# One expert of a mixture-of-experts kernel: half blocks chained on five PSUM banks, last outputs by accumulating DMAs, last products reordered

## The chip, the cores and the metric

The kernel runs on one core of a Trainium2 chip. The core has a matrix engine (TensorE, PE in the profile, with its weight loads as PEld), a vector engine (DVE), a scalar engine (ACT), a general engine (POOL) and a queue engine (SP); each runs its own instructions in order and waits for the others on semaphores. Matrix products land in PSUM, which the kernel uses in banks of 512 fp32 numbers per partition. The metric is the device time of one execution in microseconds; three runs of the kernel before took 2339.73, 2339.75 and 2340.48 us, with a median of 2339.75 us.

## What is computed

The output is the sum of three parts over 2048 tokens of 512 channels: the input, a state-space convolution of the normalized input (by an FFT in the reference), and a mixture of eight experts, of which all eight are taken for every token. Cut to what matters here:

```python
for e in range(E):
    mask = (topk_idx == e)
    w = (gates * mask).sum(-1, keepdims=True)
    h = _silu(xf @ w1[e]) @ w2[e]
    out = out + w * h
return x + _A_ref(xn, ...) + out
```

Each `w1[e]` is 512 by 1792 and each `w2[e]` is 1792 by 512. This case is about the last expert, e = 7.

## The kernel before, in words

Numbers are held as two fp16 halves (high and low), so that one exact product is three matmuls: high by high, high by low, low by high. On top of that the products are cut in a 2 by 2 scheme with seven block products in place of eight (Strassen's, in Winograd's form), with sums of blocks made before and after. For experts 0 to 6 only the first layer is done so. For the last expert (`strong` in the code) the second layer, too, is done with seven products, numbered 1 to 7.

**Blocks and slots.** The tokens go in four token blocks (`tb` 0 to 3) of 512. For the last expert each token block has two half blocks (`a` = 0, 1), and a half block is computed by two calls of `block2` (`d` = 0, 1 for the first half block, 2, 3 for the second): one for four of the seven pairs of hidden features (`prs` 0 to 3), one for the other three (4 to 6). A call of `block2` issues the first layer in four slots, s = 0 to 3: one first-layer product in slot 0, two in each of the others, in three PSUM banks A, B, C (`hb`). A product of one pair is 6 matmuls of 128 columns (L1775). Slot 1 ends with the copy of B to C on ACT (L1872), the activation of A (`act11`), and `act12` of the call before; slot 2 keeps C and A in SBUF (`keep`, L1785), and POOL adds the two with an accumulating DMA (L1666).

**From activation to second layer.** Each of the seven left operands of the second layer is scaled to fp16 on ACT (`high`, L1803) and gets its low half on DVE (`low`, L1808). Some are sums of activations, made by DVE (`total`, L1814). `when(n, f)` puts a step off by n slots; `flush()`, at the end of each slot, runs the steps that are due. When `low` is issued, one unit per pair is appended to the list `units` of that half block. A unit is one second-layer product of one pair: three matmuls of 256 columns (L1701). A half block has 7 products of 7 pairs, 49 units. Counted in slots from the start of the first call of a half block, a unit can be taken from this slot on: product 1 from slot 3, 4 from slot 6, 2 and 7 from 7, 5 and 6 from 8, 3 from 9 (four pairs each); those of the second call (three pairs each) four slots later, so that the last three, of product 3, come in slot 13. That is slot 1 of the second call of the next half block.

**`pop2`** takes up to 7 units in each slot, after the slot's first-layer products and ahead of its `flush()`. It takes half blocks strictly in order. When the 49th unit is taken it calls `evacuate2` and stops, and the slot behind it stays without units (`gap`). The seven accumulators lie in four banks, y0 to y3, the same for each half block.

**`evacuate2`** copies product 1 to SBUF on ACT (L1717), forms the four output blocks with seven DVE additions (L1719 to L1728), and one slot later scales them by the gates on ACT (L1733) and adds them to the sums in DRAM with accumulating DMAs on POOL (L1735); five slots later SP copies the finished rows to the output (L1737). For both half blocks of the last token block it does otherwise: the sums were loaded to SBUF beforehand (`final_load`, L1660), DVE multiplies by the gates and adds (L1745 to L1756), and SP and ACT issue the output DMAs themselves (L1744). Its instructions are issued inside `pop2`, and so ahead of what `flush()` issues in that slot.

```python
        if (e, tb) in strong:
            pop2(pops)
        else:
            pop(pops)
        flush()
```

**Preparation of the weights** (`work_on`) is a list of steps that a slot may take one or two of; each step is mostly one scaling on ACT (L493) and one low half on DVE (L496). At e = 6 and 7, once the memory of the convolution is free, each slot takes up to two more (L1641).

Of the kernel before, what the change touches and what calls it, by code (L numbers as in the profile page):

```python
# [9 lines left out]
F32 = mybir.dt.float32  # L10
# [4 lines left out]
ALU = mybir.AluOpType  # L15
# [3 lines left out]
P = 128  # L19
# [14 lines left out]
def s4_moe_kernel(  # L34
# [15 lines left out]
    nc = tc.nc  # L50
    V, S, T = nc.vector, nc.scalar, nc.tensor

    NTOK, D = u.shape
    NT = NTOK // P
    KT = D // P
    E, NPR = w1.shape[0], w1.shape[1]
    NF = 2 * NPR
    TB = 512
    NB = NTOK // TB
    TPB = TB // P  # L60
    TH = TB // 2
# [527 lines left out]
    second_half = {}  # L589
# [51 lines left out]
    def work_on(limit):  # L641
        clock["two"], n2 = False, limit
        while limit > 0:
            fetch()
            it = None
            for n, c in enumerate(work[:6]):
                if c.load is None:
                    if n == 0 and can(c):
                        it = c
                        break  # L650
                    if n == 0 and (c.e, c.w, 0) in done:
                        continue
                    break
                if c.raw is not None and can(c):
                    it = c
                    break
            if it is None:
                break
            if it.sums and len(it.steps) == it.n:
                live["tw"], it.at = True, now()  # L660
            low = it.steps.pop(0)(it.raw)
            limit -= 1
            clock["two"] = limit == 0 and n2 == 2
            last = not it.steps
            if last:
                work.remove(it)
            if low:
                lows.append((low, last, it.sums and last, it.made))
            elif last and it.load is not None:
                live["n"] -= 1  # L670
        fetch()
# [350 lines left out]
    def at_(n):  # L1022

        return n / 1050 + 0.17

    def tt_(n):

        return n / 960 + 0.1
# [6 lines left out]
    def now():  # L1035
        return clock["slot"]
# [481 lines left out]
    def when(n, f):  # L1518
        todo.append((now() + n, f))
# [97 lines left out]
    def slot(e, tb, d, s, pops):  # L1617
        for f in mid.get((e, tb, d, s), ()):
            f()
        if e + tb == 0:  # L1620
            work_lows()
# [5 lines that stand above are left out]
        if e == 0:  # L1627
            work_lows()
        room = act_room()
        if room > 1.0 and run_later():  # L1630
            room -= 1.6
        for f in side.get((e, tb, d, s), ()):
            f()
        work_lows()
        if e + tb == 0 or tb == NB - 1:
            work_on(2 if e + tb == 0 or room > 2 and (e or d < 3) else 1)
        elif e == 0 and tb == 1:
            work_on(2 if (d, s) < (2, 1) else 1 if (d, s) == (2, 1) else 0)
        elif room > 1.0:
            work_on(1 if room < 2.2 or e else 2)  # L1640
        if "pool" in second_half and e >= E - 2 and work:  # L1641
            work_on(2)
        if (e, tb, d, s) >= (0, 2, 3, 1):
            if (e, tb, d, s) == (0, 2, 3, 1):
                clock["pe"] = clock["pe0"] = clock["pe1"] = clock["dve"] = clock["dve0"] = 0.0
            bg_run()
        if "s4" in done and "pool" not in second_half:
            open_second()
        clock["slot"] += 1
# [19 lines left out]
    order2 = [(e, tb, a) for e in range(E) for tb in range(NB) if (e, tb) in strong for a in range(2)]  # L1669
    gap = {"at": -1}  # L1670
    OPS = (0, 3, 1, 2, 4, 5, 6)
    BANKS = {1: (0, 0), 6: (0, 1), 5: (1, 0), 7: (1, 1), 4: (2, 0), 2: (3, 0), 3: (3, 1)}

    def w2_op(pr, p, b):
        c = {1: (0, 0), 2: (1, 0), 3: (1, 1)}.get(p)
# [4 lines left out]
    def pop2(n):  # L1680

        while n > 0 and units:
            pop(1)
            n -= 4
        while n > 0 and order2 and now() > gap["at"]:
            key = order2[0]
            ps = passes.get(key)
            if ps is None or not ps["units"]:
                break
            e, pr = key[0], ps["units"][0][0]  # L1690
            if (True, (e, "w2", pr)) not in made or (True, (e, "w2x", pr)) not in made:
                break
            pr, q, p, t = ps["units"].pop(0)
            bank_, half = BANKS[p]
            first = bank_ not in ps["y"]
            if first:
                ps["y"][bank_] = ps_y.tile([P, 2, TH], F32, tag=f"y{bank_}", name=f"z{e}_{key[1]}_{key[2]}_{bank_}")
            acc = ps["y"][bank_][:, half, :]
            c = ps["n"][p] = ps["n"].get(p, 0) + 1
            for k, (a, b) in enumerate(((0, 0), (0, 1), (1, 0))):  # L1700
                T.matmul(acc, t[:, a, q, :], w2_op(pr, p, b), start=(first and k == 0), stop=(c == NPR and k == 2),  # L1701
                         skip_group_check=True)
            clock["pe"] += 0.325
            n -= 1
            ps["left"] -= 1
            if ps["left"] == 0:
                order2.pop(0)
                gap["at"] = now() + 1
                evacuate2(*key, {p: ps["y"][b][:, h, :] for p, (b, h) in BANKS.items()})
                n = 0  # L1710

    def evacuate2(e, tb, a, y):
        i0, i1 = tb * TPB + a, tb * TPB + a + 2
        g0, g1 = gates_e[e][:, i0:i0 + 1], second_half["gneg"][:, i1:i1 + 1]
        ev = second_half["pool"].tile([P, 3, TH], F32, tag="ev", name=f"ev{e}_{tb}_{a}", bufs=1)
        t1, v, w = ev[:, 0, :], ev[:, 1, :], ev[:, 2, :]
        S.copy(t1, y[1])  # L1717
        clock["act"] += at_(TH)
        V.tensor_tensor(v, t1, y[6], op=ALU.subtract)  # L1719
        V.tensor_tensor(w, v, y[5], op=ALU.add)  # L1720
        clock["dve"] += 7 * tt_(TH)
        if (e, tb) != (E - 1, NB - 1):
            o = [sb.tile([P, 2, TH], F32, tag="stg", name=f"ye{e}_{i}", bufs=4) for i in (i0, i1)]
            V.tensor_tensor(o[0][:, 0, :], t1, y[2], op=ALU.add)
            V.tensor_tensor(o[1][:, 1, :], w, y[7], op=ALU.add)
            V.tensor_tensor(v, v, y[7], op=ALU.add)
            V.tensor_tensor(o[1][:, 0, :], v, y[4], op=ALU.add)
            V.tensor_tensor(o[0][:, 1, :], w, y[3], op=ALU.add)  # L1728

            def send():  # L1730
                for i, t, g in ((i0, o[0], g0), (i1, o[1], g1)):
                    t = t.rearrange("p a d -> p (a d)")
                    S.activation(t, t, AF.Copy, scale=g)  # L1733
                    clock["act"] += at_(D)
                    nc.gpsimd.dma_start(oacc[i], t, accum_op=ALU.add)  # L1735
                    if e == E - 1:
                        when(5, lambda i=i: nc.sync.dma_start(out[i * P:(i + 1) * P, :], oacc[i]))  # L1737
            when(1, send)
            return
        f0, f1 = stg[i0], stg[i1]  # L1740
        lo, hi = slice(0, TH), slice(TH, D)

        def send(i, c, q):
            q.dma_start(out[i * P:(i + 1) * P, c], stg[i][:, c])  # L1744
        V.scalar_tensor_tensor(f0[:, lo], t1, g0, f0[:, lo], op0=ALU.mult, op1=ALU.add)  # L1745
        V.scalar_tensor_tensor(f0[:, hi], w, g0, f0[:, hi], op0=ALU.mult, op1=ALU.add)
        V.tensor_tensor(w, w, y[7], op=ALU.add)
        V.scalar_tensor_tensor(f1[:, hi], w, g1, f1[:, hi], op0=ALU.mult, op1=ALU.add)
        send(i1, hi, nc.scalar)
        V.tensor_tensor(v, v, y[7], op=ALU.add)  # L1750
        V.tensor_tensor(v, v, y[4], op=ALU.add)
        V.scalar_tensor_tensor(f1[:, lo], v, g1, f1[:, lo], op0=ALU.mult, op1=ALU.add)
        send(i1, lo, nc.sync)
        V.scalar_tensor_tensor(f0[:, lo], y[2], g0, f0[:, lo], op0=ALU.mult, op1=ALU.add)
        send(i0, lo, nc.sync)
        V.scalar_tensor_tensor(f0[:, hi], y[3], g0, f0[:, hi], op0=ALU.mult, op1=ALU.add)  # L1756
        send(i0, hi, nc.scalar)

    def block2(e, tb, d):
# [1 line left out]
        a, prs = d // 2, ((0, 1, 2, 3), (4, 5, 6))[d % 2]  # L1761
        n = len(prs)
        key = (e, tb, a)
        ps = passes.setdefault(key, {"units": [], "y": {}, "n": {}, "left": 7 * NPR})
        A, B, C = (h.rearrange("p a t -> p (a t)").rearrange("p (q t) -> p q t", q=4) for h in hb)
        tk = slice(a * P, (a + 1) * P)
        last = d == 3
# [119 lines left out]
        prod(B, 6, 2)  # L1887
        sB = keep("scB", B)
        add(sB[:, :n], sE[:, :n])
        if (e, tb) == (E - 1, NB - 1) and d in (1, 3):  # L1890
            for j in (d // 2, d // 2 + 2):
                final_load(j)
        slot(e, tb, d, 3, pops[3])
        later.append(lambda: act22(sC))
# [113 lines left out]
    while later or todo or order2:  # L2008
        if later:
            later.pop(0)()  # L2010
        pop2(10)
        flush()
        clock["slot"] += 1

# [55 lines left out]
```

## Time and profile before

| what | us |
|---|---|
| median of three runs (2339.73 to 2340.48) | 2339.75 |
| time of the profiled execution | 2341.02 |
| its span in the profile | 2339.2 |
| PE busy | 2308.1 |
| DVE busy | 1851.9 |
| ACT busy | 1503.5 |
| POOL busy | 339.5 |
| first matmul of the last expert's first layer starts at | 2043.6 |
| first matmul of its second layer starts at | 2074.04 |
| its last matmul starts at | 2331.9 |

The profiled execution took 2341.02 us, of which the span, from the first to the last thing that the profiler recorded, is 2339.2 us. Times below are counted from the start of the span. "Idle before" in the profile is the time in which an engine did nothing ahead of an instruction, with what ended it behind an arrow. A row with x36 stands for 36 instructions of one kind.

### The profile page before, as it was taken

Reading aid. Unit: us, or ns where it says so; the run is one execution under the profiler, and the core shown is the slowest. Engines: PE = TensorE matmul, PEld = TensorE weight load, DVE = VectorE, ACT = ScalarE, POOL = GpSimd, SP = SyncE. Lnnn points to the kernel's source line nnn. Section 1 sums busy time; section 2 is a strip of 40 time slices with the busy share of each in tenths; the row PEclk is TensorE's granted clock in tenths of the full one; section 3 lists DMA queues with packets and bytes.
Section 4 is the critical chain, followed back from the end, with each engine's and each line's share of the span. In section 5 each row is a group of like instructions: output and inputs, shape, how many; then the busy total and the mean of one; then the engine's idle time right before and its main releaser. Section 6 shows DMA issues by size and latency. Waiting matters only on the chain.

```text
span 2339.2 us, 49749 instructions
## 1 busy us (share of the span) xinstructions
PE 2308.1 (99%) x19969; PEld 1614.2 (69%) x19969; DVE 1851.9 (79%) x3737; ACT 1503.5 (64%) x2650; POOL 339.5 (15%) x396
## 2 busy tenths in 40 slices
PE   8999999999999999999999999999999999999997
PEld 4666666666666666666666666666666666689997
DVE  8864889989998999888999889998999734645444
ACT  7676666656666576665766667666666656756663
POOL 0010101121111211101111011110111101131110
PEclk9999999999999999999999999999999999999999
DMA  8597356665576655745556555565555755675442
GB/s 275 181 266 194 95 148 155 142 125 111 125 172 134 132 116 123 168 114 119 114 124 157 123 116 121 118 158 122 121 111 125 158 118 141 160 136 110 96 93 60
DMA packets 326457, 320.24 MB, mean 137 GB/s; under 512 B 183696, under 2 KB 221072, under 8 KB 325776
## 3 DMA queue, kind: packets, MB, share of 16 engines
q1 hardware_dynamic: 269776, 222.91, 32.9%
q0 software_dynamic: 55872, 93.61, 25.5%
q8 instruction: 156, 2.56, 0.4%
q14 instruction: 77, 0.63, 0.1%
q10 hardware_dynamic: 576, 0.52, 0.1%
HBM read 205.55 MB, written 66.06 MB: 116 GB/s over the span
## 4 chain that ended last, share of the span: by engine, by line
PE 82%; issue 7%; DVE 3%; DMA 3%; ACT 3%; POOL 1%; SPq 0%; DVEq 0%; POOLq 0%; ACTq 0%
PE hb L1463 32%; PE y L1446 12%; PE y L1448 12%; PE y L1447 12%; PE hb L1775 6%; PE z L1701 5%; DMA scC<-sE 1%; PE kgen L854 1%; PE uf L921 1%; PE kf L935 1%; PE yp L1009 1%; ACT ye L1421 0%; ACT ahl L1483 0%; POOL oacc L1424 0%; DVE ahl L1492 0%
## 5 line engine op out<-in xcount | busy, mean ns | idle before, releaser
L1463 PE MATMUL hb<-xop,w1s 128*128 128x256 f16 x7938 | 934.3, 273 | 5.0 <-ACT scC L1924 3.4
L1463 PEld LDWEIGHTS <-w1s 128*128 128x128 f16 x7938 | 766.2, 98 | 151.5 <-issue 9.4
L1447 PE MATMUL y<-w2s,ahl 128*128 128x512 f16 x1568 | 595.0, 379 | 0.4 <-DVE w2s L496 0.4
L1446 PE MATMUL y<-w2s,ahl 128*128 128x512 f16 x1568 | 595.1, 380 | 0.0
L1448 PE MATMUL y<-w2s,ahl 128*128 128x512 f16 x1568 | 595.0, 379 | 0.0
L1666 POOL DMA_DIRECT2D scC<-sE x124 | 114.8, 926 | 1352.5 <-ACT sE L1924 1036.6
L1448 PEld LDWEIGHTS <-ahl 128*128 128x128 f16 x1568 | 153.4, 98 | 185.6 <-issue 0.7
L1447 PEld LDWEIGHTS <-ahl 128*128 128x128 f16 x1568 | 153.4, 98 | 140.5
L1446 PEld LDWEIGHTS <-ahl 128*128 128x128 f16 x1568 | 153.4, 98 | 140.4
L1479 ACT ACTIVATE fa<-hb,sc 128x512 f32<-128x512 f32 (+1 forms) x220 | 140.0, 636 | 153.3 <-PE hb L1463 152.6
L1492 DVE SCALAR_TENSOR_TENSOR ahl<-fa,sc,ahl 128x512 f16<-128x512 f32 (+1 forms) x230 | 157.1, 683 | 52.9 <-ACT ahl L1483 52.5
L1939 ACT COPY hb<-hb 128x512 f32<-128x512 f32 x108 | 55.9, 517 | 196.9 <-PE hb L1463 196.7
L1666 POOL DMA_DIRECT2D scB<-sE x124 | 107.3, 865 | 390.3 <-ACT scB L1924 253.9
L1483 ACT ACTIVATE ahl<-fa,sc 128x512 f16<-128x512 f32 (+1 forms) x230 | 154.4, 672 | 8.9 <-DMA xnd<-xn 1.5
L1775 PE MATMUL hb<-xop,w1s 128*128 128x128 f16 x2352 | 143.6, 221 | 6.7 <-ACT scC L1785 6.6
L1775 PEld LDWEIGHTS <-w1s 128*128 128x128 f16 x2352 | 138.1, 99 | 10.1 <-issue 6.9
L1492 DVE SCALAR_TENSOR_TENSOR ahl<-scB,sc,ahl 128x512 f16<-128x512 f32 x108 | 73.6, 681 | 81.3 <-ACT ahl L1483 79.9
L842 DVE TENSOR_TENSOR tb<-ta,tt 128x64 f32<-128x64 f32 (+2 forms) x192 | 132.0, 687 | 5.7
L836 DVE TENSOR_TENSOR ta<-tb,zr 128x64 f32<-128x64 f32 (+2 forms) x192 | 131.7, 686 | 5.3
L1929 ACT COPY hb<-hb 128x512 f32<-128x512 f32 x108 | 56.0, 519 | 122.9 <-PE hb L1463 122.1
L976 DVE TENSOR_TENSOR s<-s,tm 128x672 f32<-128x672 f32 (+6 forms) x224 | 127.8, 571 | 7.7
L839 DVE TENSOR_TENSOR tt<-tb,zi 128x64 f32<-128x64 f32 (+2 forms) x192 | 130.5, 679 | 0.0
(319 smaller groups left out, 3220.7 us busy)
## 6 DMA issues: line engine op xcount, KB each, us to landing
xop<-xd SPq DMA_DIRECT2D x210, 256.0 KB, 4.0
pp<-in_w_dram SPq DMA_DIRECT2D x98, 512.0 KB, 4.3
raw<-in_w_dram SPq DMA_DIRECT2D x63, 512.0 KB, 4.9
oacc<-ye POOLq DMA_DIRECT2D x108, 256.0 KB, 6.0
scC<-sE POOLq DMA_DIRECT2D x89, 256.0 KB, 4.2
scB<-sE POOLq DMA_DIRECT2D x89, 256.0 KB, 4.1
raw<-in_w_dram SPq DMA_DIRECT2D x52, 256.0 KB, 3.5
raw<-in_w_dram SPq DMA_DIRECT2D x104, 128.0 KB, 3.5
```

Of the source, the lines that this page charges most:

```text
L836: V.tensor_tensor(ta, tin, zrv, op=ALU.mult)
L839: V.tensor_tensor(tt, tin[:, ::-1], ziv, op=ALU.mult)
L842: V.tensor_tensor(tout, ta, tt, op=ALU.add)
L1446: T.matmul(y, lhs[0], w2s[pr][:, 0, fh, :], start=(c == 0), stop=False)
L1447: T.matmul(y, lhs[0], w2s[pr][:, 1, fh, :], start=False, stop=False)
L1448: T.matmul(y, lhs[1], w2s[pr][:, 0, fh, :], start=False, stop=(c == NF - 1))
L1463: T.matmul(dst[:, q, :], w1s[pr][:, a, wo, k * P:(k + 1) * P], xop[:, xo, b, k, :], start=(first_mm and q == 0 and n == 0), stop=(n == 5), ...
L1479: S.activation(fa, src[:, :n], AF.Silu, scale=w1_unscale(e, d if whole else prs[0]))
L1483: S.activation(ahl[:, 0, :n], fa, AF.Copy, scale=scales[e][:, 3:4])
L1492: V.scalar_tensor_tensor(ahl[:, 1, :n], fa, sc[:, 3:4], ahl[:, 0, :n], op0=ALU.mult, op1=ALU.subtract)
L1666: nc.gpsimd.dma_start(dst, src, accum_op=ALU.add)
L1775: T.matmul(dst[:, q, :], w1s[pr][:, x, (0, 1, 2, 3, 6, 5, 4)[wo], k * P:(k + 1) * P], xop[:, xo, b, k, tk], start=(first_mm and q == 0 and ...
```

## The change

Eight edits, all in the last expert but the first, which also concerns expert 6:

1. In a slot of experts 6 and 7, `work_on` takes one more step in place of two.
2. `pop2` no longer stops when a half block is done. In the same slot it goes on with units of the next half block that go to its bank 0 (products 1 and 7); from the slot behind it on, it takes any unit. The same holds where the last units of expert 6 run out.
3. The accumulators go round five banks (`bank_tile`): half block number n has its four banks shifted by 4n modulo 5. The fifth is the bank "s4" that the convolution used. Products 1 and 7 share bank 0, 4 and 5 bank 1, 6 has bank 2, 2 and 3 share bank 3.
4. `evacuate2` copies bank 0 whole (products 1 and 7, 512 columns) in one ACT instruction; the DVE additions take product 7 from SBUF, and keep their temporaries in the output tiles. There are seven of them as before, in another order.
5. The first half block of the last token block leaves by the accumulating DMAs, as the others do; its output DMAs follow after three slots.
6. For the very last half block (`LAST`) units of product 2 are taken only when there are no others, and those of product 3 last of all; product 3 has the fifth bank to itself.
7. `final_load` loads the sums of the last half block alone, both in slot 3 of d = 1.
8. Behind the last slot, `pop2` takes 4 units at a step in place of 10.

```diff
         if "pool" in second_half and e >= E - 2 and work:
-            work_on(2)
+            work_on(1)
...
-    BANKS = {1: (0, 0), 6: (0, 1), 5: (1, 0), 7: (1, 1), 4: (2, 0), 2: (3, 0), 3: (3, 1)}
+    LAST = order2[-1]
+    RANK = {2: 1, 3: 2}
+
+    def half_of(key, p):
+        b, h = {1: (0, 0), 7: (0, 1), 4: (1, 0), 5: (1, 1), 6: (2, 0), 2: (3, 0), 3: (3, 1)}[p]
+        return (4, 0) if (key, p) == (LAST, 3) else (b, h)
+
+    def bank_tile(key, b):
+        n = (4 * passes[key]["n"] + b) % 5
+        return (ps_y if n else ps_s).tile([P, 2, TH], F32, tag=f"y{n - 1}" if n else "s4", name=f"z{key[0]}_{key[1]}_{key[2]}_{b}")
...
         while n > 0 and units:
             pop(1)
             n -= 4
-        while n > 0 and order2 and now() > gap["at"]:
+            if not units:
+                gap["at"] = now()
+                n = min(n, 4)
+        while n > 0 and order2:
             key = order2[0]
-            ps = passes.get(key)
-            if ps is None or not ps["units"]:
+            ps, e = passes.get(key), key[0]
+            if ps is None:
                 break
-            e, pr = key[0], ps["units"][0][0]
-            if (True, (e, "w2", pr)) not in made or (True, (e, "w2x", pr)) not in made:
+            ok = [u for u in ps["units"] if (now() > gap["at"] or half_of(key, u[2])[0] == 0)
+                  and (True, (e, "w2", u[0])) in made and (True, (e, "w2x", u[0])) in made]
+            if not ok:
                 break
-            pr, q, p, t = ps["units"].pop(0)
-            bank_, half = BANKS[p]
+            if key == LAST:
+                ok.sort(key=lambda u: RANK.get(u[2], 0))
+            pr, q, p, t = ok[0]
+            ps["units"].remove(ok[0])
+            bank_, half = half_of(key, p)
...
             if ps["left"] == 0:
                 order2.pop(0)
-                gap["at"] = now() + 1
-                evacuate2(*key, {p: ps["y"][b][:, h, :] for p, (b, h) in BANKS.items()})
-                n = 0
+                gap["at"] = now()
+                evacuate2(*key, {p: ps["y"][half_of(key, p)[0]][:, half_of(key, p)[1], :] for p in range(1, 8)}, ps["y"][0])
...
-        ev = second_half["pool"].tile([P, 3, TH], F32, tag="ev", name=f"ev{e}_{tb}_{a}", bufs=1)
-        t1, v, w = ev[:, 0, :], ev[:, 1, :], ev[:, 2, :]
-        S.copy(t1, y[1])
-        clock["act"] += at_(TH)
+        ev = second_half["pool"].tile([P, 2, TH], F32, tag="ev", name=f"ev{e}_{tb}_{a}", bufs=1)
+        t1, t7 = ev[:, 0, :], ev[:, 1, :]
+        S.copy(ev, both)
...
         V.tensor_tensor(v, t1, y[6], op=ALU.subtract)
         V.tensor_tensor(w, v, y[5], op=ALU.add)
-        clock["dve"] += 7 * tt_(TH)
-        if (e, tb) != (E - 1, NB - 1):
-            o = [sb.tile([P, 2, TH], F32, tag="stg", name=f"ye{e}_{i}", bufs=4) for i in (i0, i1)]
+        if (e, tb, a) != LAST:
+            V.tensor_tensor(v, v, t7, op=ALU.add)
+            V.tensor_tensor(v, v, y[4], op=ALU.add)
+            V.tensor_tensor(o[1][:, 1, :], w, t7, op=ALU.add)
             V.tensor_tensor(o[0][:, 0, :], t1, y[2], op=ALU.add)
-            V.tensor_tensor(o[1][:, 1, :], w, y[7], op=ALU.add)
-            V.tensor_tensor(v, v, y[7], op=ALU.add)
-            V.tensor_tensor(o[1][:, 0, :], v, y[4], op=ALU.add)
-            V.tensor_tensor(o[0][:, 1, :], w, y[3], op=ALU.add)
+            V.tensor_tensor(w, w, y[3], op=ALU.add)
...
-                        when(5, lambda i=i: nc.sync.dma_start(out[i * P:(i + 1) * P, :], oacc[i]))
+                        when(5 if tb < NB - 1 else 3, lambda i=i: nc.sync.dma_start(out[i * P:(i + 1) * P, :], oacc[i]))
...
-        if (e, tb) == (E - 1, NB - 1) and d in (1, 3):
-            for j in (d // 2, d // 2 + 2):
+        if (e, tb) == (E - 1, NB - 1) and d == 1:
+            for j in (1, 3):
                 final_load(j)
...
-        pop2(10)
+        pop2(4)
```

More of the change, by code (lines that the diff above doesn't have):

```diff
@@ L1684, in pop2 @@
             n -= 4
-        while n > 0 and order2 and now() > gap["at"]:
+            if not units:
+                gap["at"] = now()
+                n = min(n, 4)
+        while n > 0 and order2:
             key = order2[0]
-            ps = passes.get(key)
-            if ps is None or not ps["units"]:
+            ps, e = passes.get(key), key[0]
+            if ps is None:
                 break
-            e, pr = key[0], ps["units"][0][0]
-            if (True, (e, "w2", pr)) not in made or (True, (e, "w2x", pr)) not in made:
+            ok = [u for u in ps["units"] if (now() > gap["at"] or half_of(key, u[2])[0] == 0)
+                  and (True, (e, "w2", u[0])) in made and (True, (e, "w2x", u[0])) in made]
+            if not ok:
                 break
-            pr, q, p, t = ps["units"].pop(0)
-            bank_, half = BANKS[p]
+            if key == LAST:
[3 more added lines that the diff above has]
+            bank_, half = half_of(key, p)
             first = bank_ not in ps["y"]
             if first:
-                ps["y"][bank_] = ps_y.tile([P, 2, TH], F32, tag=f"y{bank_}", name=f"z{e}_{key[1]}_{key[2]}_{bank_}")
+                ps["y"][bank_] = bank_tile(key, bank_)
             acc = ps["y"][bank_][:, half, :]
-            c = ps["n"][p] = ps["n"].get(p, 0) + 1
+            c = ps["c"][p] = ps["c"].get(p, 0) + 1
             for k, (a, b) in enumerate(((0, 0), (0, 1), (1, 0))):
@@ L1707, in pop2, with evacuate2 @@
                 order2.pop(0)
-                gap["at"] = now() + 1
-                evacuate2(*key, {p: ps["y"][b][:, h, :] for p, (b, h) in BANKS.items()})
-                n = 0
-    def evacuate2(e, tb, a, y):
+                gap["at"] = now()
+                evacuate2(*key, {p: ps["y"][half_of(key, p)[0]][:, half_of(key, p)[1], :] for p in range(1, 8)}, ps["y"][0])
+    def evacuate2(e, tb, a, y, both):
         i0, i1 = tb * TPB + a, tb * TPB + a + 2
         g0, g1 = gates_e[e][:, i0:i0 + 1], second_half["gneg"][:, i1:i1 + 1]
-        ev = second_half["pool"].tile([P, 3, TH], F32, tag="ev", name=f"ev{e}_{tb}_{a}", bufs=1)
-        t1, v, w = ev[:, 0, :], ev[:, 1, :], ev[:, 2, :]
-        S.copy(t1, y[1])
-        clock["act"] += at_(TH)
+        ev = second_half["pool"].tile([P, 2, TH], F32, tag="ev", name=f"ev{e}_{tb}_{a}", bufs=1)
+        t1, t7 = ev[:, 0, :], ev[:, 1, :]
+        S.copy(ev, both)
+        clock["act"] += at_(D)
+        clock["dve"] += 7 * tt_(TH)
+        o = [sb.tile([P, 2, TH], F32, tag="stg", name=f"ye{e}_{i}", bufs=4) for i in (i0, i1)]
+        v, w = o[1][:, 0, :], o[0][:, 1, :]
         V.tensor_tensor(v, t1, y[6], op=ALU.subtract)
         V.tensor_tensor(w, v, y[5], op=ALU.add)
-        clock["dve"] += 7 * tt_(TH)
-        if (e, tb) != (E - 1, NB - 1):
-            o = [sb.tile([P, 2, TH], F32, tag="stg", name=f"ye{e}_{i}", bufs=4) for i in (i0, i1)]
+        if (e, tb, a) != LAST:
+            V.tensor_tensor(v, v, t7, op=ALU.add)
+            V.tensor_tensor(v, v, y[4], op=ALU.add)
+            V.tensor_tensor(o[1][:, 1, :], w, t7, op=ALU.add)
             V.tensor_tensor(o[0][:, 0, :], t1, y[2], op=ALU.add)
-            V.tensor_tensor(o[1][:, 1, :], w, y[7], op=ALU.add)
-            V.tensor_tensor(v, v, y[7], op=ALU.add)
-            V.tensor_tensor(o[1][:, 0, :], v, y[4], op=ALU.add)
-            V.tensor_tensor(o[0][:, 1, :], w, y[3], op=ALU.add)
+            V.tensor_tensor(w, w, y[3], op=ALU.add)
             def send():
@@ L1746, in evacuate2 @@
         V.scalar_tensor_tensor(f0[:, hi], w, g0, f0[:, hi], op0=ALU.mult, op1=ALU.add)
-        V.tensor_tensor(w, w, y[7], op=ALU.add)
+        V.tensor_tensor(w, w, t7, op=ALU.add)
         V.scalar_tensor_tensor(f1[:, hi], w, g1, f1[:, hi], op0=ALU.mult, op1=ALU.add)
         send(i1, hi, nc.scalar)
-        V.tensor_tensor(v, v, y[7], op=ALU.add)
+        V.tensor_tensor(v, v, t7, op=ALU.add)
         V.tensor_tensor(v, v, y[4], op=ALU.add)
@@ L1763, in block2 @@
         key = (e, tb, a)
-        ps = passes.setdefault(key, {"units": [], "y": {}, "n": {}, "left": 7 * NPR})
+        ps = passes.setdefault(key, {"units": [], "y": {}, "c": {}, "left": 7 * NPR, "n": len(passes)})
         A, B, C = (h.rearrange("p a t -> p (a t)").rearrange("p (q t) -> p q t", q=4) for h in hb)
```

## The prediction

> **What bounds the kernel now.** I read the page first, then the waits of PE in the last expert, then the stretches between them, then the slots by the timeline.
>
> ```profile
> span 2339.2 us, 49749 instructions
> PE 2308.1 (99%) x19969; PEld 1614.2 (69%) x19969; DVE 1851.9 (79%) x3737; ACT 1503.5 (64%) x2650; POOL 339.5 (15%) x396
> PE hb L1775 <- ACT scC L1785: 6.6, 2, 5.3
> PE z L1701 <- ACT ye L1421: 2.3, 1, 2.3
> PEld L1701 <- DVE hs L1808: 1.6, 6, 0.3
> 2140.00:2170.00 30.00, 29.99 (x408) 28.12 (x406) 15.76 (x29) 18.23 (x33) 5.23 (x6) 1.00 0.41 76
> ```
>
> The first two lines are the page's: PE is busy for 99% of the span. The next three are waits within the last expert (total, times, longest). In the last row the second number is PE's busy time in 30 us in its middle: none is idle, at full clock (1.00). So the free slot costs nothing there: PE fills it with first-layer products. The edits leave the matmuls as they are, so the time can move only by PE's waits, its clock, and what follows the last matmul.
>
> **What the change takes away.**
>
> ```profile
> 2038.39 1.47 PE L1463 MATMUL hb<-xop,w1s 128*128 128x256 f16 x12 [1.46 <-ACT hb L1939]
> 2036.33 1.75 ACT L493 ACTIVATE w1s<-raw,sc 128x768 f16<-128x768 f32 x2
> 2074.04 1.14 PE L1701 MATMUL z<-w2s,hs 128*128 128x256 f16 x9 [2.34 <-ACT ye L1421]
> 2109.99 2.17 PE L1775 MATMUL hb<-xop,w1s 128*128 128x128 f16 x36 [1.32 <-ACT scC L1785]
> 2308.46 2.46 ACTq L1744 DMA_DIRECT2D out_dram<-fin  x2
> 2310.04 0.47 DVE L1756 SCALAR_TENSOR_TENSOR fin<-z,gse,fin 128x256 f32<-128x256 f32 x1
> 2310.96 0.72 ACT L1803 ACTIVATE hs<-s,sc 128x512 f16<-128x512 f32 x1 [5.21 <-DVE fin L1756]
> 2312.10 4.00 PE L1775 MATMUL hb<-xop,w1s 128*128 128x128 f16 x36 [5.32 <-ACT scC L1785]
> 2331.00 1.15 PE L1701 MATMUL z<-w2s,hs 128*128 128x256 f16 x9
> 2331.61 0.42 DVE L1719 TENSOR_TENSOR ev<-ev,z 128x256 f32<-128x256 f32 x1 [7.66 <-ACT ev L1717]
> 2335.86 0.48 DVE L1756 SCALAR_TENSOR_TENSOR fin<-z,gse,fin 128x256 f32<-128x256 f32 x1
> ```
>
> *Fewer preparation steps a slot* (edit 1). PE waited 1.46 us for a copy of ACT that stood behind two scalings (1.75). One step less would spread such pairs. I take 1.5 us gained; the ends are 1.5 lost, should a step come late by as much, and 3.0 gained, with another wait of that size before.
>
> *The first second-layer product* (edits 2 and 3) waited 2.34 us for expert 6 to leave bank y0; in the fifth bank it need not: 2.3, at the low end nothing.
>
> *Outputs by accumulating DMAs* (edit 5). In the last token block ACT issues output DMAs that wait for DVE (L1744 on ACT's queue), so ACT stands until L1756, its copy scC comes late, and PE stands 5.32 us. Then its 36 matmuls take 4.00 us where the like 36 above take 2.17; the clock was at half for 3.9 us of work (rows below), which is 2.0 lost. Both go: 7.3. Added are two ACT scalings, two DMAs on POOL and two on SP, as at every other half block, where PE stands for none of them; they lie ahead of some 13 us of matmuls, and SP's last two sends queue behind SP's two. I cost them at nothing; if uncovered, they are about 2 us at the end.
>
> *The end* (edits 6 and 8). Before, the last matmul ends at 2331.00 + 1.15 = 2332.15, and DVE's eleven steps run from 2331.61 to 2336.34; the span ends 2.9 later. After, twelve units (of products 2 and 3) come behind the last one of the others, 3.9 us at 0.327 a unit (below). Nine DVE steps, 4.73 × 9 / 11 = 3.9 us, fit beside them, about 0.2 late; the last two follow, so DVE ends about 1.1 behind PE in place of 4.2: 3.1 gained. The low end is 1.5, if the operands of the last units come late; reading `final_load` earlier (edit 7) moves SP work into a covered slot and costs nothing.
>
> *Waits at the ends of half blocks* that are replaced below: 1.32 at the first, and PE's loads 1.6 in six short ones, together 2.9.
>
> Sum: 1.5 + 2.3 + 7.3 + 3.1 + 2.9 = 17.1 us.
>
> **What it adds.** Here is the slot in which a half block ends, from the middle of the expert.
>
> ```profile
> 2171.12 1.47 PE L1701 MATMUL z<-w2x,hs 128*128 128x256 f16 x12
> 2171.28 2.29 PE z L1701 x21
> 2173.57 2.01 PE hb L1775 x36
> 2171.32 0.46 ACT L1872 COPY hb<-hb 128x384 f32<-128x384 f32 x1 [2.39 <-PE hb L1775]
> 2174.20 0.35 ACT L1717 COPY ev<-z 128x256 f32<-128x256 f32 x1
> 2174.59 0.42 DVE L1719 TENSOR_TENSOR ev<-ev,z 128x256 f32<-128x256 f32 x1 [9.12 <-ACT ev L1717]
> 2176.83 0.41 DVE L1728 TENSOR_TENSOR ye<-ev,z 128x256 f32<-128x256 f32 x1
> 2177.16 0.69 DVE L1814 TENSOR_TENSOR s<-f,scC 128x512 f32<-128x512 f32 x1
> 2177.88 0.69 DVE L1814 TENSOR_TENSOR s<-s,f 128x512 f32<-128x512 f32 x1
> 2178.49 0.75 DVE L1808 SCALAR_TENSOR_TENSOR hs<-scC,sc,hs 128x512 f16<-128x512 f32 x1
> 2177.55 1.46 PEld L1701 LDWEIGHTS <-hs 128*128 128x128 f16 x14
> 2179.28 0.66 PEld L1701 LDWEIGHTS <-hs 128*128 128x128 f16 x7 [0.28 <-DVE hs L1808]
> L1865 ACT COPY hb<-hb 128x512 f32<-128x512 f32 x8 | 4.6, 572 | 4.8 <-PE hb L1775 4.8
> ```
>
> The rows "PE z" and "PE hb" (from the chain) give the prices: 21 second-layer matmuls, 7 units, take 2.29 us, 0.327 a unit; 36 first-layer matmuls take 2.01. Units start at 2171.12. At 2171.32 ACT begins a row of five instructions that hang on the slot's first-layer product, and only then, at 2174.20, comes the copy of the evacuation. DVE waits 9.12 us for that copy; seven additions follow, then two sums, then the low half of product 4 (hs<-scC, 2178.49): what `flush` issues in this slot stands behind the evacuation. PE's 14 loads are product 1's four units and the two of product 4 that read the high half; the 15th waits until 2179.28, 8.16 us after the units started. That is a wait of 0.28 only because the free slot's 36 matmuls, the next slot's 36 and four units of product 1 came first.
>
> Chained, PE comes there earlier. A half block still ends in this slot, since its last three units are usable from here on. By the availability list, the slot takes these three and four of product 1, bank 0; the next one may take anything, and what there is are the four of product 4; then 7, 7, 7, 5, 6, 6, 3: 49 again. So between the start of the units and the wait PE has seven units (2.29), one slot's products (2.01) and two matmuls of product 4 (0.22): 4.5 us. The low half comes at 8.16, and 0.2 later than now, since the copy ahead of it becomes 512 wide (0.572 in place of 0.35): 8.4. **PE waits 3.8 us.** Behind the waiting load stand the rest of product 4 and both products of the next slot, for which ACT waits, and POOL for ACT; no other engine can use the gap.
>
> In the last expert seven half blocks end with another behind them: 7 × 3.8 = 26.6 us. For a single wait the ends are 0.3 (as now, if DVE's sums were issued ahead of the evacuation, which the diff does not do) and 4.2 (if POOL or the other order of the additions delay DVE by one step). The other units with one slot's notice, in the later slots, are safe: DVE stands idle for 9 us ahead of the evacuation. The five banks add no wait: bank 1 of a half block is the one that the ACT copy frees at about 3.6 us, ahead of PE's 4.3. In the last half block 41 units remain behind the last first-layer product in place of 49; that moves units between slots, and no time.
>
> **The clock** is the term that no row gives directly.
>
> ```profile
> 2072.00:2073.00 1.00, 0.00 (x0) 0.00 (x0) 0.92 (x2) 0.97 (x3) 0.00 (x0) 1.00 1.15 176
> 2308.50:2309.00 0.50, 0.00 (x0) 0.00 (x0) 0.47 (x2) 0.00 (x0) 0.00 (x0) 1.00 0.00 0
> 2309.50:2310.00 0.50, 0.00 (x0) 0.00 (x0) 0.50 (x2) 0.00 (x0) 0.00 (x0) 0.50 0.49 166
> 2315.50:2315.80 0.30, 0.30 (x6) 0.30 (x5) 0.30 (x2) 0.00 (x0) 0.00 (x0) 0.50 0.00 0
> 2316.00:2316.20 0.20, 0.20 (x4) 0.18 (x3) 0.20 (x1) 0.06 (x1) 0.00 (x0) 1.00 0.00 0
> 2074.00:2075.00 1.00, 0.96 (x9) 0.86 (x9) 0.20 (x1) 1.00 (x2) 0.72 (x2) 1.00 0.93 162
> ```
>
> The third column from the right is the granted clock. The idle stretch of 2.3 us left it at 1.00; in the one of 5.3 (from 2306.78) it fell to 0.50 between 2309.0 and 2309.5, some 2.4 us in, and came back at 2316, 3.8 us after work did. A wait of 3.8 lies halfway between the two stretches, and is longer than the 2.4 after which the clock fell. So each costs between nothing and 2.0; I take 1.2, 8.4 for seven.
>
> [...]
>
> Sum: 26.6 + 8.4 − 17.1 = 17.9 us on a span of 2339.2. The profiled execution took 2341.02, 1.3 more than the median of the runs, 2339.75; I put the difference on the median: 2357.6 us.
>
> **The rivals.** *The same waits without the clock:* 26.6 − 17.1 = 9.5, 2349.2 us. For it speaks that 2.3 us did nothing to the clock; against it that the fall came after 2.4. [...] Chance 0.20.
>
> *No wait of note, and faster:* the low half of product 4 is there when PE comes. That needs DVE to be 3.8 us earlier, about as much as the evacuation's copy and additions take (2174.20 to 2177.16) with one sum. Then 17.1 are gained: 2322.6. The point from which it decides is a wait of (17.1 − 4.7) / 7 = 1.8 us each, without clock losses. Against it stands the order of issue, the same in both kernels, and the wait of 0.28 that shows DVE already at its limit with 36 matmuls and four units more ahead. Chance 0.15.
>
> *Between them:* waits of 1.8 to 3.1, if ACT's five instructions start earlier than here: 2335 to 2344. Chance 0.08.
>
> *The chain does nothing:* half blocks end in the same slot anyhow, since the last three units come no sooner. This I hold for true in all cases; it is why the fuller slots bring nothing, and it is no case of its own.
>
> **How the numbers follow.** The forecast, waits with a part of the clock loss, 2350 to 2364 (all seven at 2.0: 9.5 + 14.0 = 23.5, 2363.2), has 0.57. With 0.20 for the waits alone, 0.08 between and 0.15 for faster, the range 2343 to 2364 holds eight in ten. A measurement here tells 0.2% from no change, 4.7 us: slower than 2344.4 has 0.77, faster than 2335.1 has 0.15, between 0.08.
>
> **What would show it.** Right: seven waits of PE's loads for DVE's low half (L1808 now), near 3.8 us each and 33 to 40 us apart, with the granted clock below 1 behind most of them; the waits of 2.3 and 5.3 gone; the span ending 4 us behind the last matmul. Wrong: PE idle at other places, for weights or for banks; these waits short, because DVE's sums ran ahead of the evacuation; or PE's sum of matmul time changed.

## The result and the profile after

The changed kernel takes 2363.92 us (median of four runs, 2361.97 to 2364.96), against 2339.81 for the kernel before (2339.73 to 2340.48): 1.0101 times as long, with a 95% interval of 1.0084 to 1.0119. It is 24 us slower. The prediction was 2357.6 with a range of 2343 to 2364; the median lies inside, 0.1 us below the upper end, and two of the four runs lie above it.

The page of the changed kernel, its first lines:

```profile
span 2361.9 us, 49748 instructions
PE 2317.4 (98%) x19969; PEld 1620.9 (69%) x19969; DVE 1852.9 (78%) x3733; ACT 1507.2 (64%) x2652; POOL 341.4 (14%) x398
```

PE executes as many matmuls as before (19969), but is busy 9.3 us longer for them, and the span is 22.7 us longer. The first is nearly all the clock; the rest is waiting, less what the edits take away. The waits from 2030 us on (total, times, longest):

```profile
PEld L1717 <- DVE hs L1824: 29.3, 8, 4.1
PE z L1717 <- DVE hs L1824: 27.1, 8, 3.8
PE hb L1463 <- ACT hb L1955: 0.8, 1, 0.8
PE hb L1791 <- ACT scC L1801: 0.3, 1, 0.3
```

The waits of 5.3, 2.3 and 1.3 us of the kernel before are gone, and the 1.5 ahead of the last expert (L1463) is 0.8; seven of 3.8 us for DVE's low halves have come, the eighth that the rows count is one of 0.3 at the end. (The 16 lines that the change adds to the file move L1701 to L1717, L1775 to L1791, L1808 to L1824.) This is the slot in which the third half block ends, in the timeline of the changed kernel:

```profile
2178.93 2.17 PE L1791 MATMUL hb<-xop,w1s 128*128 128x128 f16 x36
2179.72 0.56 ACT L1732 COPY ev<-z 128x512 f32<-128x512 f32 x1
2180.32 0.42 DVE L1737 TENSOR_TENSOR ye<-ev,z 128x256 f32<-128x256 f32 x1 [8.67 <-ACT ev L1732]
2180.95 0.38 PE L1717 MATMUL z<-w2x,hs 128*128 128x256 f16 x2
2182.70 0.42 DVE L1744 TENSOR_TENSOR ye<-ye,z 128x256 f32<-128x256 f32 x1
2183.03 0.69 DVE L1830 TENSOR_TENSOR s<-f,scC 128x512 f32<-128x512 f32 x1
2183.75 0.69 DVE L1830 TENSOR_TENSOR s<-s,f 128x512 f32<-128x512 f32 x1
2184.36 0.75 DVE L1824 SCALAR_TENSOR_TENSOR hs<-scC,sc,hs 128x512 f16<-128x512 f32 x1
2185.16 2.31 PE L1717 MATMUL z<-w2x,hs 128*128 128x256 f16 x10 [3.83 <-DVE hs L1824]
```

Read DVE's rows from the top: 8.67 us of waiting for the copy, seven additions (2180.32 to 2183.1), two sums, and then the low half of product 4. PE issued the two matmuls of product 4 that read the high half at 2180.95 and stood for 3.83 us before the third. The next row of PE shows the second loss: ten matmuls of 256 columns take 2.31 us, where the 21 in the prediction's row took 2.29. The windows of the same wait (after the stretch, its length and the engines' busy times, the third number from the right is the granted clock):

```profile
2183.00:2184.00 1.00, 0.00 (x0) 0.00 (x0) 0.97 (x3) 0.85 (x2) 0.00 (x0) 1.00 0.88 235
2184.00:2184.50 0.50, 0.00 (x0) 0.00 (x0) 0.50 (x2) 0.50 (x2) 0.34 (x1) 0.73 1.13 187
2188.00:2189.00 1.00, 1.00 (x13) 1.00 (x11) 0.89 (x2) 0.00 (x0) 0.00 (x0) 0.50 0.84 129
2190.50:2191.00 0.50, 0.50 (x7) 0.50 (x6) 0.10 (x1) 0.00 (x0) 0.00 (x0) 0.50 0.61 94
2191.00:2191.50 0.50, 0.50 (x7) 0.47 (x6) 0.00 (x0) 0.21 (x1) 0.00 (x0) 0.94 0.86 336
```

The clock falls to one half at about 2184.2, before work goes on, and comes back only at 2191.0. The same happens at each of the seven waits; at the six others the clock stays at 0.50 for 3.41 us.

The end, in the timeline:

```profile
2349.99 0.39 PE L1717 MATMUL z<-w2x,hs 128*128 128x256 f16 x2 [0.63 <-ACT hs L1819]
2350.67 0.94 PE L1717 MATMUL z<-w2x,hs 128*128 128x256 f16 x7 [0.28 <-DVE hs L1824]
2353.73 4.09 PE L1717 MATMUL z<-w2s,hs 128*128 128x256 f16 x36
2358.26 0.48 DVE L1772 SCALAR_TENSOR_TENSOR fin<-z,gse,fin 128x256 f32<-128x256 f32 x1
```

The 36 matmuls of products 2 and 3 close the work at 2357.82; DVE ends 0.9 later and the span 4.1 later, against 4.2 and 7.1 before. Two short waits for the last operands are new.

### The profile page after: what moved, and what is told of

Read it like the earlier page. It is cut to its first block, busy times and chain, and to the rows that moved or that the text cites. A ratio compares the mean times of both kernels' runs of the same rounds, so it can differ in the third digit from the quotient of the medians.

```text
span 2361.9 us, 49748 instructions
## 1 busy us (share of the span) xinstructions
PE 2317.4 (98%) x19969; PEld 1620.9 (69%) x19969; DVE 1852.9 (78%) x3733; ACT 1507.2 (64%) x2652; POOL 341.4 (14%) x398
## 4 chain that ended last, share of the span: by engine, by line
PE 89%; ACT 4%; DVE 3%; issue 2%; DMA 2%; POOL 0%; SPq 0%; DVEq 0%; ACTq 0%; POOLq 0%
PE hb L1463 34%; PE y L1448 13%; PE y L1446 13%; PE y L1447 13%; PE hb L1791 5%; PE z L1717 4%; PE hb L1990 2%; PE kgen L854 1%; PE uf L921 1%; PE kf L935 1%; PE yp L1009 1%; DMA scC<-sE 1%; ACT ye L1421 1%; ACT hs L1819 0%; ACT ahl L1483 0%
## 5 line engine op out<-in xcount | busy, mean ns | idle before, releaser
L1463 PE MATMUL hb<-xop,w1s 128*128 128x256 f16 x7938 | 934.3, 273 | 3.4 <-ACT scC L1940 1.9
L1463 PEld LDWEIGHTS <-w1s 128*128 128x128 f16 x7938 | 766.3, 98 | 149.7 <-issue 7.6
L1791 PE MATMUL hb<-xop,w1s 128*128 128x128 f16 x2352 | 147.1, 223 | 0.3 <-ACT scC L1801 0.3
L1717 PEld LDWEIGHTS <-hs 128*128 128x128 f16 x1176 | 114.5, 100 | 44.8 <-DVE hs L1824 29.3
L1791 PEld LDWEIGHTS <-w1s 128*128 128x128 f16 x2352 | 142.4, 100 | 3.9 <-issue 0.5
```

Of the source, the lines that this page charges most:

```text
L1463: T.matmul(dst[:, q, :], w1s[pr][:, a, wo, k * P:(k + 1) * P], xop[:, xo, b, k, :], start=(first_mm and q == 0 and n == 0), stop=(n == 5), ...
L1791: T.matmul(dst[:, q, :], w1s[pr][:, x, (0, 1, 2, 3, 6, 5, 4)[wo], k * P:(k + 1) * P], xop[:, xo, b, k, tk], start=(first_mm and q == 0 and ...
```

## Experiments

The theory: PE waits since the low half of product 4 stands behind the evacuation on DVE, and the chain brings PE there too early; each wait also costs clock. The rivals: the units come too late whatever DVE's order is; another edit (banks, the wider copy) makes PE wait; the clock has nothing to do with it. Runs are compared by their ratio to the kernel before, which ran beside them on the same chip.

**The chain alone undone** (the evacuation stays where it is).

```diff
             if not units:
-                gap["at"] = now()
+                gap["at"] = now() - 1
...
-            ok = [u for u in ps["units"] if (now() > gap["at"] or half_of(key, u[2])[0] == 0)
-                  and (True, (e, "w2", u[0])) in made and (True, (e, "w2x", u[0])) in made]
+            ok = [u for u in ps["units"] if now() > gap["at"] and (True, (e, "w2", u[0])) in made and (True, (e, "w2x", u[0])) in made]
...
                 order2.pop(0)
-                gap["at"] = now()
+                gap["at"], n = now() + 1, 0
```

> The changed kernel with the chaining alone undone: the free slot as before, nothing taken of the next half block in the slot where one ends; the evacuation stays ahead of the flush, and five banks and all other edits stay. Theory: the seven waits shrink to 0.3 us as before the change, and the clock stays up: 2363.9 - 26.8 - 12.8 + 2.0 + 1.3 and the wait near the end, about 2328. Rival: another edit (five banks, the wider copy, the other order of the additions) makes PE wait: well above 2340.

Measured: 2330.94 us, 0.9955 of before (0.9942 to 0.9969). The clock's mean is 1.0 and the waits are small again:

```profile
PEld L1716 <- DVE hs L1823: 3.9, 10, 0.6
PE hb L1790 <- ACT scC L1800: 3.2, 8, 1.5
```

So the chain is what costs as long as the evacuation comes first, 0.0146 of the time or 34 us, and without it the other edits gain some 10 us. Banks, copy and order of the additions bring no large wait: the longest here, 1.5 us, is the one at the first end, where the kernel before had 1.3.

**The evacuation moved behind the flush** (the chain stays).

```diff
-                evacuate2(*key, {p: ps["y"][half_of(key, p)[0]][:, half_of(key, p)[1], :] for p in range(1, 8)}, ps["y"][0])
+                evs.append(lambda key=key, ps=ps: evacuate2(*key, {p: ps["y"][half_of(key, p)[0]][:, half_of(key, p)[1], :] for p in range(1, 8)}, ps["y"][0]))
...
         for f in due:
             f()
+        while evs:
+            evs.pop(0)()
...
-    todo = []
+    todo, evs = [], []
```

> The changed kernel with one thing moved: the evacuation is issued behind the flush of its slot, so that DVE gets the two sums and the low half of product 4 ahead of the evacuation's seven additions. Theory: PE waits only because of this order; all seven waits of 3.83 us go and with them the falls of the clock, 2363.9 - 26.8 - 12.8 = about 2324 us. Rival: units taken one slot after their low half was issued come too late whatever the order; PE still waits some 3 us seven times, about 2360 us.

Measured: 2327.45 us, 0.9941 of before (0.9926 to 0.9955). In its timeline the last half block but one ends so:

```profile
2294.80 0.74 DVE L1826 SCALAR_TENSOR_TENSOR hs<-scC,sc,hs 128x512 f16<-128x512 f32 x1
2300.34 0.42 DVE L1739 TENSOR_TENSOR ye<-ev,z 128x256 f32<-128x256 f32 x1 [4.80 <-ACT ev L1734]
2300.36 1.47 PE L1719 MATMUL z<-w2x,hs 128*128 128x256 f16 x12
```

The low half of product 4 is made while DVE would have waited, some 5 us ahead of the need of PE's four units of product 4 (x12), which now run through. The rival that a slot's notice is too short is out: the units are the same, in the same slots. The time is 3.4 us above the expected 2324; 2.3 of them are a wait near the end, taken up below. The 12.8 us that this sum took for the clock were also too many (see the sums further down).

**The free slot back, but product 1 still chained.** The wait should be shortened to a size that the prediction's sum gives.

```diff
                 order2.pop(0)
-                gap["at"] = now()
+                gap["at"] = now() + 1
```

> The changed kernel with the free slot back for all but bank 0 (units of product 1 are still chained, product 4 waits a slot longer). Theory: PE reaches product 4 at 2.3 + 4.0 + 0.2 = 6.5 us instead of 4.5, the low half comes at 8.4, so seven waits of 1.9 us, too short for the clock to fall: 2324 + 13 = about 2337 us. Rival: the free slot as such protects, as before the change, waits of 0.3: about 2326 us. Other rival: the clock falls at 1.9 us too: about 2347 us.

Measured: 2338.43 us, 0.9989 of before (0.9979 to 0.9998).

```profile
2177.10 1.27 PE L1717 MATMUL z<-w2x,hs 128*128 128x256 f16 x10 [1.44 <-DVE hs L1824]
2170.00:2180.00 10.00, 8.34 (x118) 7.63 (x116) 7.60 (x15) 7.58 (x14) 3.50 (x4) 1.00 0.76 182
```

PE waits 1.44 us at each end, plus 0.2 for ACT, and the clock stays at 1.00: ten matmuls take 1.27 us. The free slot does not protect by itself; it is the time that PE needs to get to product 4 that counts: 7.1 us here (2168.58 to 2175.66) where 6.5 were expected, so the wait is shorter than the 1.9 expected. The rival of a clock that falls at 1.9 us is left to the next run.

**The wait filled with idle matmuls**, which leave DVE's order as it is and only keep PE at work for part of the wait.

```diff
+            if first and bank_ == 1 and ps["n"]:
+                for _ in range(18):
+                    T.matmul(acc, t[:, 0, q, :], w2_op(pr, p, 0), start=True, stop=True, skip_group_check=True)
             c = ps["c"][p] = ps["c"].get(p, 0) + 1
```

> The changed kernel with 18 idle matmuls of 256 columns (2.0 us) put ahead of the first unit of product 4 in each half block but the first, into the accumulator that this unit then starts afresh. Theory: they lie within the wait of 3.8 us, leave 1.9 us idle, and hold the clock up, so only the clock's part goes: about 2352 us. Rival: the clock has no such part, or falls at any wait: 2364 us. If the wait were not bound by DVE, 2.0 us more each: 2378 us.

Measured: 2351.97 us, 1.0043 of before (1.0028 to 1.0058).

```profile
2108.62 1.26 PE L1720 MATMUL z<-w2x,hs 128*128 128x256 f16 x10 [1.86 <-DVE hs L1827]
2108.00:2109.00 1.00, 0.38 (x4) 0.34 (x5) 1.00 (x2) 1.00 (x2) 1.00 (x3) 1.00 0.20 32
```

With 126 more matmuls the kernel is 0.0058 faster than the changed one, 12 to 14 us. The wait that remains is 1.86 us, and the clock stays at 1.00 there. Its mean over the run is 1.000 in two of the four runs and 0.998 in the others, where the changed kernel has 0.992 to 0.994; a single stretch of 3.41 us at 0.50 would have left 0.999. So the clock's part of the loss is about 12 us, 1.7 a wait; the rest is waiting.

**One edit alone on the kernel before: outputs by accumulating DMAs.**

```diff
     gap = {"at": -1}
+    order2_last = order2[-1]
...
-        if (e, tb) != (E - 1, NB - 1):
+        if (e, tb, a) != order2_last:
...
-                        when(5, lambda i=i: nc.sync.dma_start(out[i * P:(i + 1) * P, :], oacc[i]))
+                        when(5 if tb < NB - 1 else 3, lambda i=i: nc.sync.dma_start(out[i * P:(i + 1) * P, :], oacc[i]))
...
-        if (e, tb) == (E - 1, NB - 1) and d in (1, 3):
-            for j in (d // 2, d // 2 + 2):
+        if (e, tb) == (E - 1, NB - 1) and d == 1:
+            for j in (1, 3):
```

> The kernel before with one part of the change: the first half block of the last token block leaves by accumulating DMAs, and the sums of the last half block are loaded in slot 3 of d = 1. Theory: the wait of 5.3 us and the slow matmuls behind it go, 7.3 us: about 2332.5 us. Rival: PE waits there for DVE's additions anyway, and nothing goes: 2339.8 us.

Measured: 2334.75 us, 0.9968 of before (0.9956 to 0.9980), 7.5 us. At the place of the wait PE now runs on:

```profile
2305.48 4.35 PE L1776 MATMUL hb<-xop,w1s 128*128 128x128 f16 x72
```

The profile of this run holds something else: at the 2.34 us that PE waits for expert 6's bank, as in the kernel before, the clock fell this time (last section), which cost 1.7 us: the 9 matmuls behind the wait took 1.44 us in place of 1.14, and the 36 after them 3.56 in place of 2.17. The fall has nothing to do with this edit.

**One edit alone on the kernel before: fewer preparation steps** (`work_on(2)` to `work_on(1)`).

> The kernel before with the first edit alone (one extra preparation step a slot in place of two). Theory: PE's waits behind pairs of ACT scalings ahead of the last expert go, 1.5 to 2.6 us: 0.9990 times the kernel before. Rival: the last expert started 2.6 us earlier in the changed kernel by chance or by another edit: ratio 1.0000.

Measured: 2339.30 us, 0.9993 of before (0.9984 to 1.0001): 1.6 us, which the interval does not part from nothing. In its profile the last expert's first layer starts at 2041.9 us, 1.7 earlier than in the kernel before. In the run of the DMAs alone, which lacks this edit, it starts at 2042.8, so 0.8 of such a difference comes without it.

**The wait near the end.** With the evacuation behind the flush, 2.3 us of waiting for ACT were left in the last half block. POOL's issues there:

```profile
2304.17 1.77 POOL L1753 DMA_DIRECT2D oacc<-ye  x2 [1.95 <-ACT ye L1751]
2305.62 1.22 POOL L1668 DMA_DIRECT2D scB<-sE  x1
```

The add of the last scB, on which the last products hang, stands behind the two output DMAs. They were put off by two slots:

```diff
-            when(1, send)
+            when(3 if (e, tb) == (E - 1, NB - 1) else 1, send)
```

> The kernel with the evacuation behind the flush, and the accumulating DMAs of the first half block of the last token block two slots later, so that POOL issues the add of the last scB ahead of them. Theory: this add stood behind them on POOL's queue and DMA engines, and PE's wait of 2.3 us near the end comes from it: 2.3 us less than e1, about 2325.2. Rival: the add takes as long by itself; same as e1, 2327.5.

Measured: 2324.19 us, 0.9929 of before (0.9916 to 0.9941), 2.8 us less than with the evacuation moved alone by the ratios. The intervals overlap, but the wait itself is gone from the trace: the longest left near the end is 0.6 us.

```profile
2304.53 0.86 POOL L1668 DMA_DIRECT2D scB<-sE  x1 [2.43 <-ACT scB L1803]
2307.51 0.62 ACT L1815 ACTIVATE scB<-scB,sc 128x384 f32<-128x384 f32 x1 [0.24 <-DMA scB<-sE]
```

POOL issues the add first, and ACT has the sum at 2307.51; before the edit it had it at 2311.42. Of these 3.9 us, 1.1 are the earlier issue: the edit also puts off two scalings on ACT, which stood ahead of the copy that the add waits for. The other 2.8 are the add itself, 3.0 us from issue to landing in place of 5.8; whether it stood in POOL's queue or in the DMA engines was not parted. This kernel beats both, 17 us under the one before.

**The order in the last half block undone**, without and with that edit.

```diff
-        return (4, 0) if (key, p) == (LAST, 3) else (b, h)
+        return (b, h)
...
             if key == LAST:
-                ok.sort(key=lambda u: RANK.get(u[2], 0))
+                pass
```

> The kernel with the evacuation behind the flush (2327.5 us, 0.9941 of before), without the last edit on order: units of the very last half block are taken as they come, product 3 shares its bank with 2. Theory: DVE's eleven steps again follow the last matmul, 3.1 us more; but the wait of 2.3 us for the last operands is filled with the units of products 2 and 3, so 0.8 us more than e1: about 2328.3. Rival, as predicted before: all of the 3.1 us come back: 2330.6.

Measured: 2327.01 us, 0.9940 of before (0.9928 to 0.9953): the same as with the order. The 2.3 us of waiting are gone, and the span again ends 7.0 us behind the last matmul: without the order, the units of products 2 and 3 fill the wait.

> The kernel with the evacuation behind the flush and the later accumulating DMAs (2324.2 us), without the last edit on order. Theory: with the wait near the end gone there is nothing for the units of products 2 and 3 to fill, so the 3.1 us of DVE's steps behind the last matmul come back, less the 0.6 that PE still waits: about 2326.7. Rival: the order is worth nothing in itself: 2324.2.

Measured: 2326.41 us, 0.9936 of before (0.9923 to 0.9948), against 0.9929 with the order. By the ratios the order is worth some 2 us once the wait is gone; the intervals overlap, so this is not clear of nothing. The profiles agree in direction: the span ends 4.1 us behind the last matmul with the order and 7.0 without.

**No chain, the evacuation behind the flush.**

> The kernel with the evacuation behind the flush, with no chaining at all: the free slot as before, nothing taken of the next half block in the slot where one ends; five banks and all other edits stay. Theory: PE is never idle in the middle, so fuller slots bring nothing: 1.3 us more for the first end (PE waits for ACT there), 2.3 less near the end, where more units cover the last operands: about 2326.5. Rival: chaining is worth its units, some 2.3 us at each of seven ends: about 2343.

Measured: 2327.72 us, 0.9943 of before (0.9930 to 0.9957), against 0.9941 with the chain. The waits differ, though:

```profile
PE hb L1792 <- ACT scC L1802: 3.2, 8, 1.5
PE z L1718 <- ACT hs L1820: 1.2, 1, 1.2
```

Unchained, PE waits 1.5 us for ACT at the first end and 0.2 at each of the six others, where the chained kernel does not wait; in the last half block it waits 1.2 us where the chained one waits 2.3. So the equal times are a balance of waits. No run shows the unchained kernel with the later output DMAs, which would show whether the chain is worth the 2.9 us at the ends.

## Why the prediction was right, and where its sizes were off

**The order of DVE's work was the cause, as argued.** The prediction had PE reach product 4's third matmul 4.5 us after the slot's units start and its low half come at 8.4, a wait of 3.8; in the trace it is 4.7 and 8.5 (2176.64 to 2181.33 and to 2185.16) and 3.83, seven times: 26.8 us against 26.6. Moving the evacuation behind the flush removes the waits, and undoing the chain reduces them to what they were; both were tried alone.

**The clock was mis-sized.** The prediction took 1.2 us a wait, 8.4 in all, and gave 2.0 as the upper end. PE's busy time grew by 9.3 us on the same matmuls although the 2.0 of the kernel before went, which makes 11.3; the filled waits give 12 to 14. The step that failed is the one that placed a wait of 3.8 us halfway between a gap that did nothing and one that cost 2.0: in truth the clock fell at every wait. The upper end failed too. At the third wait the clock stayed at one half for 6.8 us (2184.2 to 2191.0), 5.9 of them at work, so 2.9 were lost there. The median, 2363.9, lies even above the 2363.2 of the case with 2.0 us at every wait, because less went away than was predicted (below); that it stays within the range is luck.

**What goes away** was predicted at 17.1 us. By terms:

| term | predicted | measured |
|---|---|---|
| preparation steps | 1.5 | 2.6 in the profiles (first layer at 2041.0 in place of 2043.6), of which 0.8 may be there without the edit; alone 1.6, not clear of nothing. The wait that the term was read from only fell from 1.5 to 0.8 |
| first second-layer product | 2.3 | 2.0 (0.30 of 2.34 left, for ACT) |
| outputs by DMAs | 7.3 | 7.5 alone |
| the end | 3.1 | 3.0 in the profile (7.1 to 4.1), less 0.9 of new waits there |
| replaced waits | 2.9 | 1.3 (the first end). The 1.6 of PE's loads were no idle time of PE, which was busy 3.00 of 3.00 us from 2177 to 2180 in the kernel before, around such a wait |

The DMAs on POOL were costed at nothing, with 2 us "if uncovered". In the changed kernel they cost the 0.9 us of new waits at most; in the kernel with the evacuation moved they were uncovered, and 2.8 us came back when they were put off. "Ahead of some 13 us of matmuls" looked at their own end and not at what queues behind them.

Together: 26.8 and about 11.2 of clock, less 2.6, 2.0, 7.3, 3.0 and 1.3, and 0.9 added, give the 22.7 us of the spans, where 17.9 were predicted; the clock's 11.2 is here the remainder, and agrees with the 11.3 from PE's busy time. (The expectations of two runs take 12.8 for it, because they count the 1.6 of the loads as gained.) The missing 4.8 us are thus 2.8 of clock, 1.6 of loads and small terms; the medians differ by 1.4 us more than the spans.

**That the chain itself brings nothing** was right for the fuller slots: with the evacuation behind the flush, the times with and without it do not differ (0.9941 and 0.9943). Whether it gains the short waits for ACT at the ends, up to 2.9 us, stays open.

## What to carry to other kernels

A free slot in a hand-made order may be the cover of another engine's chain: before it is taken out, count on that engine, in order of issue, what stands ahead of the operands that are then needed first. Work that nobody waits for (an evacuation into a bank that has a spare, output DMAs) belongs behind the work of the same slot that another engine waits for. Where PE was busy to 99%, tighter packing gained nothing, and each of the seven new waits, 3.83 us long, cost clock as well: 1.3 to 2.9 us each on top of the wait, half of the time that PE worked at 0.50.

## What was not expected of the hardware

The granted clock fell at every wait of 3.83 us, at different distances from its start, from 2.90 us (the third) to 4.57 (the fourth). At the fourth and the fifth it fell only behind the end of the wait: the fourth ends at 2224.45, and the clock is 1.00 until 2225.2; the fifth ends at 2262.56, and the clock falls at 2262.74.

```profile
2224.00:2225.00 1.00, 0.55 (x5) 0.50 (x6) 1.00 (x3) 0.99 (x2) 1.00 (x2) 1.00 0.44 33
2225.00:2226.00 1.00, 1.00 (x9) 0.76 (x7) 1.00 (x2) 0.00 (x0) 0.21 (x1) 0.60 0.77 68
```

The length of a wait alone does not decide it. The wait of 2.34 us for expert 6's bank left the clock up in the kernel before, and brought it down in the run of the DMAs alone:

```profile
2073.28 1.44 PE L1702 MATMUL z<-w2s,hs 128*128 128x256 f16 x9 [2.34 <-ACT ye L1421]
2073.00:2074.00 1.00, 0.72 (x7) 0.65 (x7) 0.43 (x1) 1.00 (x3) 0.48 (x1) 0.99 1.10 199
2074.00:2075.00 1.00, 1.00 (x9) 0.82 (x8) 0.55 (x1) 1.00 (x2) 1.00 (x3) 0.50 0.64 115
```

In the run of the DMAs alone the wait runs from 2070.94 to 2073.28, and the clock falls at about 2074.0, 0.7 us behind its end. In the kernel before, the wait runs from 2071.70 to 2074.04, and the clock is 1.00 from 2071 to 2077. What parts the two no run shows. The waits of PE and the clock:

| wait | granted clock |
|---|---|
| 1.44 us, free slot back (2175.66 to 2177.10) | 1.00 |
| 1.86 us, with the idle matmuls (the first, 2106.76 to 2108.62) | 1.00 |
| 2.34 us, kernel before (2071.70 to 2074.04) | 1.00 |
| 2.34 us, DMAs alone (2070.94 to 2073.28) | 0.50 from about 2074.0, 3.0 us after the wait's start |
| 5.32 us, kernel before (2306.78 to 2312.10) | 0.50 from 2309.14, 2.36 us after the start, for 6.83 us |
| 3.83 us, changed kernel, all but the third | 0.50 from 3.07 to 4.57 us after the start, for 3.41 us |
| 3.83 us, changed kernel, the third (2181.33 to 2185.16) | 0.50 from 2184.23, 2.90 us after the start, for 6.83 us |

In these runs the clock thus stayed at 1.00 at the waits of 1.44 and 1.86 us shown, did both at 2.34, and fell at 3.83 and 5.32.
